# Decayed linear attention and two expert layers on one core: whole chunks of 128 on the halves of the TensorE array, operands in PSUM, and the first expert tile transposed earlier

## The chip, the cores and the metric

One Trainium2 chip, one of its cores. The metric is the device time of one execution of the whole program in microseconds; the kernel before was timed in three runs. TensorE (PE) multiplies, its weight loads are listed as PEld; VectorE is DVE, ScalarE is ACT, GpSimd is POOL, SyncE is SP. Each engine works through its own queue in order. Almost all transfers are issued from SP's queue; the indexed gathers and scatters from POOL's.

## The reference

Three stages follow each other. The inputs are 4 sequences x 8 heads x 768 tokens x 48 features.

```
state = alpha[t][:, None] * state + k[t][:, None] * v[t]     # per head, 48 x 48, token by token
y[t]  = q[t] @ state
x = y, heads side by side                                    # 3072 x 384
# first expert layer: every token goes to one of 8 experts
e = argmax(x @ w_gate + bias[modality]);  g = softmax weight of e
x = g * (relu(x @ w1[e]) @ w2[e])                            # 384 -> 1024 -> 384
# second expert layer: only tokens with x @ w_skip > 0
out = x + (relu(x @ w1b[e2]) @ w2b[e2])                      # else out = x
```

## The kernel before

**Attention.** The 3,072 tokens are 24 chunks of 128 (`SPB` = 6 to a sequence). The decay is turned into a running product `b` over the chunk (`scan`), so that a chunk needs only matrix products: `qmul` is q times b, and `lnexp`, `kmul`, `newton` and `kb` give k divided by b (the reciprocal by `Ln` and `Exp` on ScalarE and one Newton step on VectorE). Features lie on partitions, one head of a pair on 0 to 47 (`EV`), the other on 64 to 111 (`OD`), four pairs (`g`) side by side, so that every such operation has 128 partitions x 512 elements. `scores` multiplies kb with qb in two halves of 64 tokens, `masks` zeroes what lies ahead in time, `umm` gives the update of the state (to 64 and to 128 tokens), `state` subtracts it, `decay` multiplies by the chunk's last b, `scopy` copies the states. `ymm` forms y of 64 tokens in one product: the masked scores and the scaled q lie above each other in X and Y, v and the state in RX and RY; that is why v is also loaded a second time in another order (`vy`). `yout` copies y and stores it, `xpose`, `xcopy`, `logits` and `lgcopy` make the gate's logits of the first expert layer.

**The order.** The program is scheduled by hand: `FIRST` lists the calls of the first chunks, and `BODY` the calls of one step t, where `("scores", 2, 0)` works on chunk t-2. There are 22 listed steps (t from 4 to 25) and a tail written out behind them. An engine's queue holds its instructions in that order.

**Sort steps.** In the background of attention the tokens are sorted by expert, in batches of columns (a column is one chunk's 128 tokens): `BATCH1` gives first column, number of columns and the step at which a batch is put on the list. A batch chooses the expert of each token, ranks the tokens (`rank`), computes gate weights and builds two one-hot matrices for each column (`onehot`), whose product (`place`) writes the token numbers into the expert's rows of a table. Each `("tick",)` in `BODY` runs the list on by one `yield`, mostly one small VectorE instruction. `early` reads the table after the first batches, `early_rows` gathers the first tile's 256 rows.

**Weights.** `split` separates the fp32 weights of the first expert, loaded during attention, into a high part (ScalarE copy) and a low part (a subtraction); `side` does an eighth in a step. **Expert layers.** A branch (`ok_reg`) stands behind the attention, with a plain version of it that these inputs don't need. Then a loop over tiles of 256 tokens: gather, six transposes, split of the rows into high and low part (`lp.xpose`), three products for each of w1 and w2, scatter to `out` and `x2_d`. In its first tile the last batch of the sort runs in the background (`rest`, `turns`). The second layer works on tiles of 128.

Of the kernel before, what the change touches and what calls it, by code (L numbers as in the profile page):

```python
# [38 lines left out]
BODY = [
    ("ktr", 2), ("scan", 0), ("kcopy", 2), ("load_v", 0), ("decay",), ("kmul", 1), ("newton", 1), ("xpose", 4), ("load", -2), ("warm",),  # L40
    ("scores", 2, 0), ("xcopy", 4), ("qmul", 1), ("tick",), ("umm", 2), ("tick",), ("scores", 2, 1), ("guards", 1), ("ymm", 3, 0),
    ("lnexp", 0), ("state", 2), ("kb", 1), ("tick",), ("ymm", 3, 1), ("side", True), ("masks", 2, 0), ("masks", 2, 1), ("scopy", 2),
    ("logits", 4), ("yout", 3), ("tick",), ("start", -1), ("tick",), ("side", False), ("tick",), ("lgcopy", 4), ("hook",),
# [3 lines left out]
    ("load", 0), ("zero", "wz"), ("zero", "D1[0]"), ("warm", 12), ("clear", 0), ("load", 1), ("hook", -1), ("load_v", 0),  # L47
    ("zero", "D1[1]"), ("load", 2), ("start", 0), ("scan", 0), ("zero", "guard"), ("zero", "ups"), ("clear", 1), ("decay", -1),
    ("lnexp", 0), ("kmul", 0), ("newton", 0), ("kb", 0), ("start", 1), ("scan", 1), ("qmul", 0), ("clear", 2), ("warm", 5), ("ktr", 0),
    ("kcopy", 0), ("scores", 0, 0), ("load", 3), ("lnexp", 1), ("scores", 0, 1), ("masks", 0, 0), ("load_v", 1), ("umm", 0), ("qmul", 1),  # L50
    ("load_v", 2), ("kmul", 1), ("newton", 1), ("kb", 1), ("masks", 0, 1), ("state", 0), ("start", 2), ("scan", 2), ("warm", 6),
    ("load", 4), ("ktr", 1), ("decay", 0), ("kcopy", 1), ("scopy", 0), ("lnexp", 2), ("scores", 1, 0), ("scores", 1, 1), ("umm", 1),
    ("qmul", 2), ("zero", "m1"), ("zero", "wg"), ("guards", 2), ("masks", 1, 0), ("gate",), ("guards", 1), ("masks", 1, 1), ("ymm", 0, 0),
    ("kmul", 2), ("newton", 2), ("ymm", 0, 1), ("kb", 2), ("start", 3), ("guards", 0), ("load_v", 3), ("load", 5), ("state", 1),
# [6 lines left out]
def attention(tc, ctx, qka, vn, vy, wg1, x_d, ident, mask, lg, guard, ups, wz, hook, side, tick):  # L61
# [81 lines left out]
    def scores(i, c):
        if c == 0:
            st[i]["sc"] = ps.tile([P, NP, 2, CH], F32, name="sc")
        sc = st[i]["sc"]
        cs = slice(c * CH, c * CH + CH)
        for g in range(NP):
# [1433 lines left out]
```

## Time and profile before

| | |
|---|---|
| median of 3 runs | 651.57 us (650.91 to 653.29) |
| profiled execution, own time | 654.04 us |
| its span, first to last instruction | 652.3 us |
| PE busy | 589.5 us (90%) |
| DVE busy | 415.7 us (64%) |
| ACT busy | 286.1 us (44%) |
| POOL busy | 321.9 us (49%) |
| mean granted TensorE clock | 0.967 |

The attention takes the first 200 us or so, the first expert layer the stretch to about 475 us, the second the rest. Shares over the whole span mix three stages with different limits; the table is only the frame.

### The profile page before, as it was taken

How to read it: one execution, taken by the hardware profiler on the slowest of the kernel's cores; microseconds unless marked ns; L12 is line 12 of the kernel's file. 1: busy time of each engine (PE TensorE's matmuls, PEld its weight loads, DVE VectorE, ACT ScalarE, POOL GpSimd, SP SyncE). 2: the span in 40 equal slices, each digit the busy share in tenths (PEclk: the TensorE clock that was granted, in tenths of full speed). 3: DMA queues.
4: the chain of work that ended last, by engine and by line, in shares of the span. 5: the costliest groups of instructions: out<-in, count | busy, mean ns of one | idle time of the engine just before them, and what ended most of it. 6: DMA issues, size and time to landing. Idle time of an engine off the chain costs nothing. (4 is left out here: it accounts for less than half of the span.)

```text
span 652.3 us, 16532 instructions
## 1 busy us (share of the span) xinstructions
PE 589.5 (90%) x5491; PEld 539.5 (83%) x5498; DVE 415.7 (64%) x965; ACT 286.1 (44%) x563; POOL 321.9 (49%) x336
## 2 busy tenths in 40 slices
PE   6779897877897899999999999999879999999994
PEld 3668776776786799999999999999868878888894
DVE  8999999999967632454483443434476657547531
ACT  2756576656623122222442223222442838357521
POOL 5767687557624323424274432245335556437432
PEclk8978999989979899999999999999999999999998
DMA  8866799977511262214276422233001394807010
GB/s 263 203 148 160 173 272 309 209 197 196 160 34 35 55 226 73 72 38 143 66 228 206 134 68 68 76 116 106 28 15 46 124 307 165 302 30 236 28 34 26
DMA packets 42927, 87.64 MB, mean 134 GB/s; under 512 B 10032, under 2 KB 29714, under 8 KB 42788
## 3 DMA queue, kind: packets, MB, share of 16 engines
q1 hardware_dynamic: 35364, 65.87, 35.8%
q0 software_dynamic: 7424, 20.25, 9.2%
q8 instruction: 47, 0.77, 0.5%
q14 instruction: 92, 0.75, 0.4%
HBM read 65.86 MB, written 22.84 MB: 136 GB/s over the span
## 5 line engine op out<-in xcount | busy, mean ns | idle before, releaser
L797 PE MATMUL yp<-w2h,l_hh 128*128 128x384 f32 x336 | 102.3, 351 | 0.0
L1279 PE MATMUL hp<-l_x,w1h 128*128 128x256 f32 x624 | 99.9, 285 | 0.1
L797 PE MATMUL yp<-w2l,l_hh 128*128 128x384 f32 x336 | 98.7, 340 | 0.0
L797 PE MATMUL yp<-w2h,l_hl 128*128 128x384 f32 x336 | 98.2, 340 | 0.0
L1285 DVE SCALAR_TENSOR_TENSOR l_hl<-hp,l_hh 128x512 fp32r<-128x512 f32 x52 | 35.7, 686 | 88.8 <-ACT l_hh L1284 53.5
L1279 PEld LDWEIGHTS hp<-l_x,w1h 128*128 128x128 f32 x624 | 84.9, 190 | 0.7 <-issue 0.5
L710 POOL DMA_INDIRECT x_d<-ys,ti x24 | 25.1, 1046 | 100.9 <-DVEq L1230 55.5
L1284 ACT ACTIVATE l_hh<-hp 128x512 fp32r<-128x512 f32 x52 | 31.1, 599 | 92.9 <-PE hp L1279 79.8
L797 PEld LDWEIGHTS yp<-w2h,l_hh 128*128 128x128 f32 x336 | 61.0, 190 | 2.1 <-ACT l_hh L702 0.9
L797 PEld LDWEIGHTS yp<-w2h,l_hl 128*128 128x128 f32 x336 | 62.7, 190 | 0.0
L797 PEld LDWEIGHTS yp<-w2l,l_hh 128*128 128x128 f32 x336 | 60.9, 188 | 0.1
L1412 PE MATMUL hp<-w1h,l_x 128*128 128x512 f32 x192 | 54.0, 403 | 2.9 <-ACTq L1363 2.8
L1341 ACT ACTIVATE ys<-yp,l_gt 128x384 f32<-128x384 f32 x26 | 15.2, 584 | 89.3 <-PE yp L797 30.0
L1279 PE MATMUL hp<-l_x,w1l 128*128 128x256 f32 x312 | 53.9, 281 | 0.0
L201 PE MATMUL yp<-RX,X 128*64 128x48 f32 x384 | 47.3, 237 | 0.1
L703 DVE TENSOR_TENSOR l_hl<-tp,l_hh 128x512 fp32r<-128x512 f32 x32 | 22.1, 691 | 38.7 <-ACT l_hh L702 35.2
L202 PE MATMUL yp<-RY,Y 128*64 128x48 f32 x384 | 46.3, 232 | 0.0
L1415 ACT ACTIVATE hs<-hp 128x512 f32<-128x512 f32 x32 | 19.2, 599 | 60.3 <-PE hp L1412 60.1
L149 PE MATMUL sc<-X,kb 64*64 64x64 f32 x384 | 34.1, 234 | 12.2 <-DVE Y L155 10.5
L1279 PEld LDWEIGHTS hp<-l_x,w1l 128*128 128x128 f32 x312 | 44.5, 190 | 0.0
L149 PEld LDWEIGHTS sc<-X,kb 64*64 64x64 f32 x384 | 28.0, 144 | 19.9 <-POOL X L123 12.6
L123 POOL TENSOR_TENSOR Y<-qka,bt 48x512 f32<-48x512 f32 x24 | 43.4, 1807 | 1.8
(263 smaller groups left out, 1433.0 us busy)
## 6 DMA issues: line engine op xcount, KB each, us to landing
qka<-in_qka_dram SPq DMA_DIRECT2D x40, 288.0 KB
ring<-in_w1b_dram SPq DMA_DIRECT2D x5, 1536.0 KB
ring<-in_w2b_dram SPq DMA_DIRECT2D x5, 1536.0 KB
x_d<-xg SPq DMA_DIRECT2D x12, 385.0 KB
vn<-in_vn_dram SPq DMA_DIRECT2D x24, 192.0 KB
x_d<-xs SPq DMA_DIRECT2D x24, 192.0 KB
ring<-in_w2b_dram SPq DMA_DIRECT2D x4, 768.0 KB
qka<-in_qka_dram SPq DMA_DIRECT2D x3, 768.0 KB
```

What stands on the lines that cost most here:

```text
L123: nc.gpsimd.tensor_tensor(out=T[i % 4][r], in0=st[i]["q"][r], in1=st[i]["b"][r], op=MUL)
L149: nc.tensor.matmul(sc[OR:P, g, c], lhsT=st[i]["kb"][:OR, g, cs], rhs=X[i % 4][:OR, g, cs], start=True, stop=True)
L201: nc.tensor.matmul(yp[cs, 2 * g], lhsT=X[i % 4][:, g, cs], rhs=RX[i % 4][:, c, g], start=True, stop=True)
L202: nc.tensor.matmul(yp[cs, 2 * g + 1], lhsT=Y[i % 4][:, g, cs], rhs=RY[i % 4][:, c, g], start=True, stop=True)
L703: nc.vector.tensor_tensor(out=lo, in0=src, in1=hi.bitcast(F32), op=SUB)
L710: nc.gpsimd.indirect_dma_start(out=out, out_offset=bass.IndirectOffsetOnAxis(ap=idx, axis=0), in_=rows, in_offset=None, bounds_check=N - 1 ...
L797: nc.tensor.matmul(yp, lhsT=h[:, f, js], rhs=w[:, f], start=(f, i) == (0, 0), stop=(f, i) == last)
L1279: nc.tensor.matmul(hp[:, g], lhsT=w[:, c, f * P : (f + 1) * P], rhs=x[:, c], start=(i == 0), stop=(i == len(terms) - 1))
L1284: nc.scalar.activation(lp.hh[:, fs], hp, AF.Relu)
L1285: nc.vector.scalar_tensor_tensor(out=lp.hl[:, fs], in0=hp, scalar=0.0, in1=lp.hh[:, fs].bitcast(F32), op0=MAX, op1=SUB)
L1412: nc.tensor.matmul(hp[g], lhsT=a, rhs=b, start=(i == 0), stop=(i == 3 * DC - 1))
L1415: nc.scalar.activation(hs[:, g * 512 : (g + 1) * 512], hp[g], AF.Relu)
```

## The change

The attention works on whole chunks of 128 tokens. `scores` is eight products of 48 x 128 by 48 x 128, the even head of a pair on rows 0 to 63 of the array and the odd one on rows 64 to 127, and one mask product of 1,024 elements follows. y is formed transposed, with features on partitions, in one PSUM bank `yT`: `yheld` multiplies the held state with qb, `yadded` adds v times the masked scores. The gate's logits are taken from there (`logits` in four column groups, `ltcopy`, and `lturn`, which sums the four and turns them), and `xpose` turns y back into rows for storing. X, Y, RX, RY, the second copy of v, `clear` and `scopy` are gone; `umm` and `state` are made once for the chunk. `D1` and `r0` lie in PSUM, each with one buffer, `newton` writes over `r0`, and `kmul` is on VectorE. Logits go into the bank that also holds `ups`.

The order in `BODY` is new. One-hot matrices have 8 buffers, and `place` no longer runs within the ticks: columns are collected and multiplied by `("place",)` a step later; a batch pauses (`STEP`) until the next step after its count. The batches are 8, 8, 6 and 2 columns. `early` needs the first 8 alone. The batch of 6 is only ranked within attention, its one-hots are made in `rest`, ahead of the batch of 2. The low parts of the splits go to GpSimd, and `side` covers 16 eighths of w1 and w2. The first expert tile is transposed and split in the attention's tail (`first_rows`), ahead of the branch. `x2_d` is `x_d`, without the zero fill.

```
-WARM = (12, 5, 6, 8, 4, 2, 2) + (0,) * 18 + (2, 0, 0)
+WARM = (12, 5, 6, 8, 4, 2, 2) + (0,) * 21
 BODY = [
...
+    ("warm",), ("scores", 2), ("place",), ("qmul", 1), ("side", False), ("scan", 0), ("ktr", 2), ("kcopy", 2), ("load_v", 0), ("state", 3),
+    ("decay",), ("logits", 4), ("ltcopy", 4), ("kmul", 1), ("newton", 1), ("kb", 1), ("load", -2), ("yheld", 3), ("guards", 1), ("xpose", 4),
+    ("lturn", 4), ("yout", 4), ("lgcopy", 4), ("tick",), ("tick",), ("umm", 2), ("lnexp", 0), ("masks", 2), ("tick",), ("tick",), ("tick",),
+    ("tick",), ("yadded", 3), ("start", -1), ("side", True), ("ycopy", 3), ("hook",), ("done", 4),
 ]
...
-    D1 = bufs("D1", [P, NP, P], 2)
-    RX, RY = bufs("RX", [P, 2, NP, DH], 4), bufs("RY", [P, 2, NP, DH], 4)
+    D1 = ps.tile([P, NP, P], F32, name="D1")
+    yT = ps.tile([P, NP, P], F32, name="yT")
...
-        for R, r in ((RX, slice(OR, P)), (RY, slice(0, OR))):
-            nc.sync.dma_start(out=R[i % 4][r].rearrange("p c g e -> p (c g e)"), in_=vy[i, r])
...
-        r0 = st[i]["r0"] = wk.tile([P, NP, P], F32, name="r0")
+        r0 = st[i]["r0"] = ps.tile([P, NP, P], F32, name="r0")
...
-        (nc.vector if i < 3 else nc.gpsimd).tensor_tensor(out=k0, in0=st[i]["k"], in1=st[i]["r0"], op=MUL)
+        nc.vector.tensor_tensor(out=k0, in0=st[i]["k"], in1=st[i]["r0"], op=MUL)
...
-        for T, r in ((X, EV), (Y, OD)):
-            nc.gpsimd.tensor_tensor(out=T[i % 4][r], in0=st[i]["q"][r], in1=st[i]["b"][r], op=MUL)
+        t = st[i]["qb"] = wk.tile([P, NP, P], F32, name="qb", bufs=4)
+        nc.gpsimd.tensor_tensor(out=t, in0=st[i]["q"], in1=st[i]["b"], op=MUL)
...
-        nt = st[i]["nt"] = wk.tile([P, NP, P], F32, name="nt")
-        nc.vector.tensor_tensor(out=nt, in0=st[i]["b"], in1=st[i]["r0"], op=MUL)
+        nc.vector.tensor_tensor(out=st[i]["r0"], in0=st[i]["b"], in1=st[i]["r0"], op=MUL)
...
+    HEADS = [(g, par, (EV, OD)[par]) for g in range(NP) for par in range(2)]
+    def scores(i):
+        sc = st[i]["sc"] = ps.tile([P, 2, NP, P], F32, name="sc")
+        for g, par, d in HEADS:
+            nc.tensor.matmul(sc[:, par, g], lhsT=st[i]["kb"][d, g], rhs=st[i]["qb"][d, g], start=True, stop=True)
+    def masks(i):
+        t = st[i]["A"] = wk.tile([P, 2 * NP, P], F32, name="A")
         nc.vector.tensor_tensor(
+            out=t, in0=st[i]["sc"].rearrange("p r g t -> p (r g) t"), in1=mask.unsqueeze(1).to_broadcast([P, 2 * NP, P]), op=MUL
         )
...
+        for g, par, d in HEADS:
+            nc.tensor.matmul(up[d, g], lhsT=kbt[:, g, d], rhs=v[:, par, g], start=True, stop=True)
...
+    def yheld(i):
+        for g, par, d in HEADS:
+            nc.tensor.matmul(yT[d, g], lhsT=st[i]["S"][d, g], rhs=st[i]["qb"][d, g], start=g == 0, stop=False)
+    def yadded(i):
+        for g, par, d in HEADS:
+            nc.tensor.matmul(yT[d, g], lhsT=st[i]["v"][:, par, g], rhs=st[i]["A"][:, par * NP + g], start=False, stop=g == NP - 1)
+    def ycopy(i):
+        t = st[i]["yt"] = wk.tile([P, NP, P], F32, name="yt")
+        nc.scalar.copy(t[:DR], yT[:DR])
...
+            nc.tensor.matmul(lpt[32 * g : 32 * g + E], lhsT=wg[:DR, g], rhs=st[i]["yt"][:DR, g], start=True, stop=True)
+    def ltcopy(i):
+        t = st[i]["lt"] = wk.tile([P, P], F32, name="lt")
+        nc.scalar.copy(t, lpt)
+    def lturn(i):
+        nc.tensor.matmul(st[i]["xq"][:, 0, DR : DR + E], lhsT=st[i]["lt"], rhs=fold, start=True, stop=True)
...
-        for e, T, r in ((nc.gpsimd, RX[i], slice(32, OR)), (nc.gpsimd, RY[i], slice(96, P)), (nc.vector, X[i], slice(32, OR)), (nc.vector, Y[i], slice(96, P))):
-            e.memset(T[r], 0.0)
...
     a, z = NS - 2, NS - 1
+    place()
+    logits(a)
...
+    tick(8)
+    w = ps.tile([P, 2, NP, P], F32, name="sc")
+    first_rows([flat(w[:, r]) for r in range(2)])
...
-BATCH1 = ((0, 8, 13), (8, 8, 19), (16, 4, 24), (20, 4, NCOL + 4))
-EARLY = 2
+BATCH1 = ((0, 8, 12), (8, 8, 20), (16, 6, 25), (22, 2, NCOL + 4))
+EARLY = 1
...
-    x2_d = dr.tile([N, XW], F32, name="x2_d")
+    x2_d = x_d
...
-            while work:
+            while work and not held:
                 try:
-                    next(work[0])
+                    if next(work[0]) == STEP:
+                        held.append(1)
                     break
...
+    def places():
+        held.clear()
+        while columns:
+            place1(columns.pop(0))
...
-        if FT + 5 <= t < FT + 13:
-            wt.split(0, wt.one, parts=(t - FT - 5,), of=8, pool_parts=(), high=high, low=not high)
+        i = t - FT - (5 if high else 6)
+        if 0 <= i < 16:
+            wt.split(i // 8, wt.one, parts=(i % 8,), of=8, pool_parts=range(8), high=high, low=not high)
...
-        if 12 <= t < 24:
-            i = 2 * (t - 12)
-            nc.sync.dma_start(out=x2_d.rearrange("(p n) d -> p n d", p=P)[:, i : i + 2], in_=xg[1])
...
+            yield from onehots1(*BATCH1[-2][:2])
+            steps = batch(*BATCH1[-1][:2], [t[:, :64], tot])
...
-        lp.xpose(0, meanwhile)
-        wt.split(1, wt.one, parts=(1, 2), pool_parts=range(3))
+        turns(TU1)
+        i = NCOL + 1 - FT - 5 - 8
+        wt.split(1, wt.one, parts=(i,), of=8, pool_parts=range(8), high=False)
+        wt.split(1, wt.one, parts=range(i + 1, 8), of=8, pool_parts=range(8))
         turns(TU2)
```

## Rows read from the trace of the kernel before

**Rows 1.** Busy us (instructions) in stretches: PE, PEld, DVE, ACT, POOL; clock, DMA.

```profile
40.00:60.00 20.00, 17.63 (x271) 15.90 (x273) 18.46 (x24) 13.29 (x32) 14.70 (x12) 0.74 0.56 135
100.00:120.00 20.00, 16.55 (x302) 14.76 (x301) 19.88 (x39) 13.20 (x31) 13.70 (x10) 0.91 1.01 274
208.00:228.00 20.00, 17.24 (x116) 16.40 (x117) 14.32 (x59) 4.33 (x9) 9.80 (x10) 0.91 0.21 44
228.00:248.00 20.00, 20.00 (x151) 19.84 (x150) 6.31 (x24) 5.28 (x11) 5.26 (x9) 1.00 0.56 207
```

**Rows 2.** Single lines, 60 to 160 us: ns minimum/median/maximum, first and last start.

```profile
L102 DVE TENSOR_SCALAR D<-qka x13: 152/281/1262, 66.9 to 155.4; 128x4 f32<-128x4 f32 x13
...
L106 DVE TENSOR_TENSOR_SCAN bt<-qka,D x13: 1204/1212/2306, 67.2 to 158.0; 128x512 f32<-128x512 f32 x13
...
L127 DVE TENSOR_TENSOR nt<-bt,r x14: 654/660/1701, 59.7 to 159.2; 128x512 f32<-128x512 f32 x14
...
L132 DVE SCALAR_TENSOR_TENSOR kb<-nt,k x13: 673/683/1562, 62.1 to 153.0; 128x512 f32<-128x512 f32 x13
...
L155 DVE TENSOR_TENSOR X<-sc,call x13: 695/695/695, 64.4 to 153.9; 64x512 f32<-64x512 f32 x13
```

**Rows 3.** Order in time, GpSimd and VectorE: start us, us, instruction.

```profile
107.10 1.27 POOL L123 TENSOR_TENSOR X<-qka,bt 48x512 f32<-48x512 f32 x1
...
107.15 1.26 DVE L102 TENSOR_SCALAR D<-qka 128x4 f32<-128x4 f32 x1
```

**Rows 4.** Order in time, VectorE: the sixth and the last scan of 24.

```profile
38.41 1.22 DVE L106 TENSOR_TENSOR_SCAN bt<-qka,D 128x512 f32<-128x512 f32 x1
...
172.74 1.22 DVE L106 TENSOR_TENSOR_SCAN bt<-qka,D 128x512 f32<-128x512 f32 x1
```

**Rows 5.** Costliest groups: count, busy us, mean ns of one, idle before.

```profile
L1285 DVE SCALAR_TENSOR_TENSOR l_hl<-hp,l_hh 128x512 fp32r<-128x512 f32 x52 | 35.7, 686 | 88.8 <-ACT l_hh L1284 53.5 <-ACTq L1230 34.4 <-issue 0.9
```

**Rows 6.** Order in time, VectorE: one pair of one-hots.

```profile
181.72 0.27 DVE L527 TENSOR_SCALAR s_S<-call,s_lo 128x128 f16<-128x128 f32 x1
181.92 0.36 DVE L529 TENSOR_SCALAR s_R<-call,s_col 128x192 f16<-128x192 f32 x1
```

**Rows 7.** Order in time, TensorE: scores, y, gate, transposes, and last the update product.

```profile
102.13 0.27 PE L149 MATMUL sc<-X,kb 64*64 64x64 f32 x1
...
102.59 0.22 PE L149 MATMUL sc<-X,kb 64*64 64x64 f32 x1
...
103.24 0.28 PE L201 MATMUL yp<-RX,X 128*64 128x48 f32 x2
...
103.48 0.32 PE L201 MATMUL yp<-RX,X 128*64 128x48 f32 x4
...
103.75 0.28 PE L201 MATMUL yp<-RX,X 128*64 128x48 f32 x2
...
104.55 0.94 PE L221 MATMUL xq<-wg1s,xt 128*128 128x128 f32 x6
105.55 0.57 PE L137 MATMUL kp<-call,kb 112*128 112x112 f32 x4
...
190.82 1.06 PE L169 MATMUL sb<-vn,kbt 64*48 64x48 f32 x32
```

**Rows 8.** Groups of ScalarE: a copy of the states (RY's is the second).

```profile
L188 ACT COPY RX<-S 48x384 f32<-48x384 f32 x24 | 12.2, 507 | 9.3 <-DVE S L174 9.3
```

**Rows 9.** Groups of VectorE: one of the two clears of a buffer.

```profile
L230 DVE MEMSET X<- 32x512 f32 x4 | 1.9, 485 | 0.6 <-issue 0.5
```

**Rows 10.** Order in time behind attention: the branch, the first tile, the second's transposes.

```profile
204.79 0.19 DVE L988 TENSOR_TENSOR s_L<-lg,sel 128x32 f32<-128x32 f32 x1 [2.07 <-DVEq L1081]
...
208.00 0.59 PE L1279 MATMUL hp<-l_x,w1h 128*128 128x256 f32 x3
...
214.45 0.24 PE L533 MATMUL acc<-s_R,s_S 128*128 128x192 f16 x1 [2.01 <-DVE s_R L529]
...
225.99 0.82 PE L776 MATMUL px<-call,xg 128*128 128x128 f32 x6
```

More of the change, by code (lines that the diff above doesn't have):

```diff
@@ L44 @@
 ]
 FIRST = [
[L47 to L54, printed above, removed]
@@ L55 @@
-    ("yout", 0), ("scopy", 1), ("scan", 3), ("clear", 3), ("warm", 8), ("lnexp", 3), ("hook", 0), ("start", 4),
+    ("load", 0), ("zero", "wz"), ("zero", "D1"), ("warm", 12), ("load", 1), ("hook", -1), ("load_v", 0),
+    ("load", 2), ("start", 0), ("scan", 0), ("zero", "guard"), ("zero", "ups"), ("zero", "yT"), ("decay", -1),
+    ("lnexp", 0), ("kmul", 0), ("newton", 0), ("kb", 0), ("start", 1), ("scan", 1), ("qmul", 0), ("warm", 5), ("ktr", 0),
+    ("kcopy", 0), ("scores", 0), ("load", 3), ("lnexp", 1), ("masks", 0), ("load_v", 1), ("umm", 0), ("qmul", 1),
@@ new lines @@
+    ("load_v", 2), ("kmul", 1), ("newton", 1), ("kb", 1), ("state", 0), ("start", 2), ("scan", 2), ("warm", 6),
+    ("load", 4), ("ktr", 1), ("decay", 0), ("kcopy", 1), ("lnexp", 2), ("scores", 1), ("umm", 1),
+    ("qmul", 2), ("zero", "m1"), ("zero", "wg"), ("guards", 2), ("masks", 1), ("gate",), ("guards", 1), ("yheld", 0), ("yadded", 0),
+    ("kmul", 2), ("newton", 2), ("kb", 2), ("start", 3), ("guards", 0), ("load_v", 3), ("load", 5),
+    ("ycopy", 0), ("scan", 3), ("warm", 8), ("lnexp", 3), ("hook", 0), ("start", 4),
@@ L143, in scores @@
[L143 to L148, printed above, removed]
-            nc.tensor.matmul(sc[OR:P, g, c], lhsT=st[i]["kb"][:OR, g, cs], rhs=X[i % 4][:OR, g, cs], start=True, stop=True)
-            nc.tensor.matmul(sc[:OR, g, c], lhsT=st[i]["kb"][OR:, g, cs], rhs=Y[i % 4][OR:, g, cs], start=True, stop=True)
-    def masks(i, odd):
-        T, r = ((X, slice(OR, P)), (Y, slice(0, OR)))[odd]
+        nc.scalar.copy(t, st[i]["kp"][:, :, :DR])
@@ L249, in gate @@
     def gate():
-        nc.sync.dma_start(out=wg[:, :, :E], in_=wg1.rearrange("(c p) e -> p c e", p=P))
+        w = wg1.rearrange("(g r e) n -> r e g n", r=2, e=DH)
+        for par, d in enumerate((EV, OD)):
+            nc.sync.dma_start(out=wg[d], in_=w[par])
     for e in FIRST:
         dict(locals())[e[0]](*e[1:])
-    base = dict(ktr=2, kcopy=2, scan=0, lnexp=0, start=-1, load=-2, load_v=0, xpose=4)
-    ops = dict(ktr=ktr, kcopy=kcopy, scan=scan, lnexp=lnexp, start=start, load=load, load_v=load_v, kmul=kmul, newton=newton, scores=scores, ymm=ymm, umm=umm, guards=guards, kb=kb, qmul=qmul, logits=logits, state=state, scopy=scopy, yout=yout, masks=masks, lgcopy=lgcopy, xpose=xpose, xcopy=xcopy)
+    base = dict(ktr=2, kcopy=2, scan=0, lnexp=0, start=-1, load=-2, load_v=0, ycopy=3)
+    ops = dict(ktr=ktr, kcopy=kcopy, scan=scan, lnexp=lnexp, start=start, load=load, load_v=load_v, kmul=kmul, newton=newton, scores=scores, yheld=yheld, yadded=yadded, umm=umm, guards=guards, kb=kb, qmul=qmul, logits=logits, state=state, ycopy=ycopy, yout=yout, masks=masks, lgcopy=lgcopy, ltcopy=ltcopy, lturn=lturn, xpose=xpose, done=done)
     for e in BODY:
@@ L279, in attention @@
     a, z = NS - 2, NS - 1
+    place()
+    logits(a)
+    ltcopy(a)
+    yheld(z)
     xpose(a)
-    xcopy(a)
-    ymm(z, 0)
-    ymm(z, 1)
-    yout(z)
-    warm(TAIL[0])
-    logits(a)
-    lgcopy(a)
-    hook(NS + 2)
-    tick(nt)
-    xpose(z)
-    xcopy(z)
-    warm(TAIL[1])
-    logits(z)
-    lgcopy(z)
-    tick(nt)
+    lturn(a)
+    yadded(z)
+    lgcopy(a)
+    yout(a)
+    ycopy(z)
+    tick(8)
+    w = ps.tile([P, 2, NP, P], F32, name="sc")
+    first_rows([flat(w[:, r]) for r in range(2)])
+    hook(NS + 2)
+    logits(z)
+    ltcopy(z)
+    xpose(z)
+    lturn(z)
+    lgcopy(z)
+    place()
+    tick(8)
+    yout(z)
     hook(NS + 3)
@@ L706 @@
 ET = mybir.EngineType
+STEP = "step"
 def put(nc, out, idx, rows):
@@ L1050, in hook @@
             first_loads()
+        if t == NCOL + 1:
+            check.append(fast_ok(one))
+            next(check[0])
         if t == NCOL + 2:
-            fast_ok(one)
+            now(check[0])
         if t == NCOL + 3:
```

185 lines of the change are left out of this document (81 added, 104 removed).

## The prediction

> **What bounds the kernel now.** I read the stretches first, then single lines, then the order in time. In the attention steps VectorE is the full engine: 19.88 of 20 us, with TensorE at 16.55, ScalarE at 13.20 and GpSimd at 13.70; from 208 us on TensorE is full and VectorE is at a third [rows 1]. So until about 200 us a microsecond off VectorE counts, and afterwards only TensorE's time does.
>
> Next is what VectorE does with its time. The same instruction has a minimum and a maximum far apart: the 4-element start 152 to 1262 ns, the scan 1204 to 2306, `newton`'s product 654 to 1701, `kb` 673 to 1562. The mask product, whose one operand is in PSUM, took 695 ns thirteen times out of thirteen [rows 2]. The order in time shows the cause: GpSimd's `qmul` began at 107.10 and took 1.27 us; VectorE's start began at 107.15 and ended 0.04 us after it [rows 3]. An instruction that takes all its operands from SBUF stands still while GpSimd works; one with a PSUM operand does not. The sixth scan begins at 38.41 us and the last at 172.74: 18 steps in 134.3 us, 7.46 us each [rows 4].
>
> **VectorE's part of a step.** D1 and r0 move to PSUM, so start, scan, `kmul`, `newton` and `kb` each keep at most one SBUF input. I price them at their undisturbed times: start 0.15, scan 1.21, `newton` and `kb` 0.69 each [rows 2]. 0.69 is also what the 512-element product on a PSUM operand takes in the expert stage [rows 5]. `kmul` comes from GpSimd: plus 0.69. The two mask products become one of 1,024 elements: 0.69 + 512 more at (0.695 - 0.152)/508 = 1.07 ns each = 1.24. Of the two state subtractions one stays: 192 elements, 0.15 + 0.20 = 0.35. Sum 0.15 + 1.21 + 3 x 0.69 + 1.24 + 0.35 = 5.0 us. Bounds of the PSUM form: not dearer than the minimum (4.9 in all), or the mask's 35 ns over `newton`'s minimum on each of the five (5.2). I take 5.0.
> [...]
>
> Between these sit the sort's small steps: 16 one-hot pairs at about 0.49 from start to start [rows 6], some 50 others near 0.2 (estimate; none is longer than a one-hot undisturbed). About 14 us of them fall into the 18 steps, some 9 of which carry them: +1.5 us there, and +0.3 where GpSimd still holds one of them up. VectorE then needs 5.0 (4.6 to 5.0, since starts overlap ends by 0.07) in an empty step and 6.4 in a loaded one. The weight splits' low halves go to GpSimd, hidden: it then has `qmul` 1.27, decay and one split of 384 elements, about 3 us of a step (an estimate).
>
> **TensorE's part.** Each fp32 matmul is two records. In scores two quadrants run at once: 8 pairs in 0.46 us, 0.066 a pair [rows 7]. With 128 columns a pair takes 0.13: scores 1.05, `yheld` the same 1.05. The update product halves, 1.06 to 0.53. Two sets of four transposes: 2 x 0.57. `lturn` 0.25 (estimate: two of the gate products' 0.125). Gate product now: six of 128 columns in 0.94, so (0.94 - 0.32)/5 = 0.125 each, with 0.32 the length of one. `yadded` streams 128 columns through 48 weight columns, 16 x 0.125 = 2.0 us one after the other, or 1.0 if the even and odd heads' column halves overlap. One place shows such an overlap: where the first column half meets the second, 8 records take 0.27 us, against 4 in 0.24 just before [rows 7]. The new gate products go to four column groups: 8 x 0.125 = 1.0, or 0.25. Sum 1.05 + 1.05 + 0.53 + 1.14 + 0.25 + (1.0 to 2.0) + (0.25 to 1.0) = 5.3 to 7.0 us, against 16.55/20 x 7.46 = 6.2 now. I take 5.9, near the overlapped end, because rows show overlap in both directions.
> One wait is new here. The gate products write the bank that `state` reads, so `logits` of chunk t-4 waits until `state` of chunk t-3 is done, 1.6 us into VectorE's step. Behind it in TensorE's order stand `yheld`, the transposes, `lturn`, `umm` and `yadded`, 4.0 us at the chosen rates: they end 5.6 us into the step, and the next scores need the mask before them anyway. It hides in a step of 6 us and sets the floor at about that; I put empty steps at 6.0.
>
> **ScalarE's part** is now 13.20/20 x 7.46 = 4.9 us [rows 1]. The state copies (2 x 0.51) and one more copy of 384 elements, as long, go [rows 8]; a copy of 512 elements (0.65 by length), one of 128 (0.2) and half a microsecond of high split more often come, estimates by length: about 4.8. r0 has one buffer now, so `Ln` of chunk t waits for `kb` of chunk t-1, 3.6 us into the step; behind it on ScalarE are the high split and `ycopy`, for which only the next step's gate product waits. `Ln` and `Exp` end at 3.7 + 1.26 = 5.0, and `kmul` asks for them at one step + 1.6: hidden while a step is above 3.5 us.
>
> **Sum of the steps.** Empty steps at that 6.0, loaded ones at VectorE's 6.4, mean 6.2; +0.2 because the clock is at its lower level in parts (0.74 in one stretch [rows 1]) and TensorE has less slack to hide it. 18 x (7.46 - 6.4) = **19 us**.
>
> **Startup.** The eight VectorE clears (0.485 each [rows 9] and up to 0.15 until the next, 5 us), one D1 memset (0.5) and some 4 us of stretched operations (an estimate: four that take the maxima of [rows 2] for the minima) go; yT's memset (0.5) and two `kmul` (1.4) come: **7.5 us**. `load_v`'s two extra transfers leave SP's queue, which nothing waited for; counted at nothing. So do the twelve zero fills.
>
> **Step 23 to the first expert product**: now 208.00 - 172.74 = 35.3 us [rows 4, 10]. After: rest of step 23 6.4; step 24, with no scan but 12 sort steps, 6.4; step 25 to its mask 2.8; then VectorE has 8 one-hot operations (2.2), 8 ranking steps (1.7), the first tile's two low halves (1.1), and count to gate weights (2.5): 7.5; the branch 2.07 [rows 10]. Total 25.2: **10 us** less. The six transposes of the first tile, after the branch now, stand ahead of it.
>
> **First expert tile**, 208.00 to 225.99. It waits 2.01 us for a one-hot operation that GpSimd's weight split holds up, and at 0.91 of the clock loses 1.8 us [rows 1, 10]. GpSimd's share drops from two parts of 1,024 elements to about three of 384. But eight columns' one-hots (before: four) now come in the background, some 8 steps later, so the index is ready about 3 us later and the gather of the second tile may show. Net **3 us**, bounds 0 and 4.
>
> **No change elsewhere**: 13 first-layer and 16 second-layer tiles. With the first batch alone (1,024 tokens) the first expert needs 256 tokens; the reference's own inputs route 483 there, so no tile is added. x2 shares x's rows now; gather and scatter of one tensor are ordered among each other, but stand several us apart on GpSimd's queue.
>
> Sum: 19 + 7.5 + 10 + 3 = 39.5. Against the profiled execution's 654.04 that is 614.5; the median of the runs is 2.5 lower, so **612 us**.
>
> **Rivals.**
> *TensorE becomes the bound* (column halves do not overlap): 7.0 a step instead of 6.4, 18 x 0.6 = 11 us, 623. The single place of overlap in the rows is thin evidence: 0.22.
> [...]
> *The second tile's gather is late*: `placed` runs 8 steps longer, 3 us of index plus two gathers; the first tile gains nothing and loses 4 more: 619. 0.10.
> *Nothing is gained on VectorE*, that is, GpSimd holds up PSUM forms too: a step is 7.46 - 0.34 - 0.15 + 0.69 (+ up to 0.5) = 7.7 to 8.2, 4 to 13 us lost in the steps, 20 gained around them: 635 to 644. Against it: thirteen masks without a spread; for it: no scan with a PSUM operand is shown. 0.08.
> [...]
> [...] 0.04.
> My forecast holds 0.56. Slower by over 0.5% (what a measurement of this kernel can just tell from no change) comes from the last rival alone, same from the edge of the one before: faster 0.93, same 0.03, slower 0.04.
>
> **Range.** Lower end: TensorE at 5.3 and VectorE never held up, 5.7 a step: 18 x 0.7 = 12.6 less, 600. Upper end: TensorE at 7.0 and the gather late: 623 + 7 = 630.
>
> **What would show it.** Scans at 1.21 without spread; steps of 6.2 to 6.6 us; masks as one operation of 1.24; the last scan near 146 us, the first expert product near 171, the second tile's transposes near 186; 13 and 16 tiles. Wrong, if TensorE is full from 30 to 150 us, if VectorE's forms with PSUM still spread, or if the second tile waits for its rows.

## The result and the profile after

The changed kernel takes 618.63 us (median of 4 runs, 617.63 to 619.74), the kernel before 651.24 on the same chip (649.91 to 653.29): a ratio of 0.9497 (95% interval 0.9465 to 0.9529). The forecast was 612.0, its range 600 to 630. The profiled execution took 617.63 us (span 615.9, mean granted clock 0.974), 36.4 less than the profiled one of before. One execution of the study, the profiled one of `rows_behind_branch`, was a slow one and is not counted in its ratio (with it the median of its four runs is 614.01 us). By the places at which the prediction cut the program (only the fourth stretch ends later than there, behind the second tile's transposes and not ahead of them):

| stretch | before | after | gained | predicted |
|---|---|---|---|---|
| start to the sixth scan | 38.41 | 27.24 | 11.2 | 7.5 |
| sixth scan to the last, 18 steps | 134.33 | 107.79 | 26.5 | 19 |
| last scan to the first expert product | 35.26 | 30.53 | 4.7 | 10 |
| to the second half of the first tile's second products | 18.56 | 22.08 | -3.5 | 3 |
| the rest | 425.7 | 428.3 | -2.5 | 0 |

The forecast of the median is 6.6 us off. The sum is 3.1 us off (39.5 predicted, 36.4 measured) because errors of 2.5 to 7.5 us in all five terms nearly cancelled. The other 3.5 us come from the profiled executions: the prediction put the median 2.5 us under the profiled execution, and after the change it lies 1.0 above it. What has to be explained is the terms.

The scans that bound the 18 steps, in the order of time of VectorE after (against [rows 4]):

```profile
27.24 1.21 DVE L101 TENSOR_TENSOR_SCAN bt<-qka,D 128x512 f32<-128x512 f32 x1
...
135.03 1.22 DVE L101 TENSOR_TENSOR_SCAN bt<-qka,D 128x512 f32<-128x512 f32 x1
```

The busy time by stretches after, columns as in [rows 1]:

```profile
40.00:60.00 20.00, 19.41 (x316) 15.99 (x314) 18.65 (x37) 13.66 (x38) 7.01 (x10) 1.00 0.91 206
...
100.00:120.00 20.00, 19.73 (x307) 16.66 (x306) 19.55 (x38) 14.85 (x40) 8.23 (x10) 0.93 0.73 167
...
160.00:180.00 20.00, 12.65 (x85) 11.63 (x85) 13.64 (x59) 3.61 (x9) 3.85 (x4) 0.66 0.09 15
```

TensorE and VectorE are now both nearly full in the steps, and GpSimd's 13.7 us of 20 have become 8. The third line is the branch and most of the first expert tile: no engine is full there, and the clock is at 0.66 on average: it is granted at 0.50 from 162 to 174 us and at 1.00 from 176 us on.

Single VectorE lines after, 27 to 160 us, minimum, median and maximum in ns (against [rows 2]):

```profile
L97 DVE TENSOR_SCALAR D<-qka x18: 153/156/168, 31.7 to 134.8; 128x4 f32<-128x4 f32 x18
...
L101 DVE TENSOR_TENSOR_SCAN bt<-qka,D x19: 1214/1221/1222, 27.2 to 135.0; 128x512 f32<-128x512 f32 x19
...
L122 DVE TENSOR_TENSOR r<-bt,r x20: 686/690/692, 29.2 to 141.7; 128x512 f32<-128x512 f32 x20
...
L127 DVE SCALAR_TENSOR_TENSOR kb<-r,k x20: 691/692/692, 29.9 to 142.4; 128x512 f32<-128x512 f32 x20
...
L154 DVE TENSOR_TENSOR A<-sc,call x21: 1197/1215/1221, 30.5 to 149.4; 128x1024 f32<-128x1024 f32 x21
```

The spread is gone: minimum and maximum lie within 25 ns, where they lay up to 1.1 us apart. An empty step in TensorE's order after (against [rows 7]):

```profile
60.67 1.16 PE L149 MATMUL sc<-qb,kb 48*128 48x128 f32 x16 [0.54 <-DVE D L97]
61.76 0.60 PE L133 MATMUL kt<-call,kb 112*128 112x112 f32 x4
62.31 0.41 PE L202 MATMUL sb<-yt,wg1s 112*8 112x128 f32 x8
62.65 1.08 PE L180 MATMUL yT<-qb,S 48*48 48x128 f32 x16
63.66 0.60 PE L133 MATMUL kt<-call,yt 112*128 112x112 f32 x4
64.10 0.30 PE L210 MATMUL kt<-call,lt 128*128 128x8 f32 x2
64.33 0.56 PE L161 MATMUL sb<-vn,kbt 128*48 128x48 f32 x16
64.72 1.05 PE L185 MATMUL yT<-A,vn 128*48 128x128 f32 x16
```

From 60.67 to the next scores at 65.70 TensorE never stops: 5.0 us a step, where the prediction took 5.9. Around the branch after, in TensorE's order (against [rows 10]):

```profile
159.06 0.40 PE L202 MATMUL sb<-yt,wg1s 112*8 112x128 f32 x8 [2.30 <-DVE nok L957]
...
165.56 0.98 PE L1310 MATMUL hp<-l_x,w1h 128*128 128x256 f32 x3 [5.13 <-DVEq L1107]
...
169.47 0.32 PE L525 MATMUL acc<-s_R,s_S 128*128 128x192 f16 x1 [1.14 <-DVE s_R L521]
...
187.12 0.76 PE L768 MATMUL px<-call,xg 128*128 128x128 f32 x5 [1.01 <-DMA xg<-x_d,l_gi]
```

The last gate product waits 2.30 us for the capacity check `nok`, whose sum lies in its PSUM bank; TensorE then stands 5.13 us before the branch; in the tile it waits for one-hots, and at the end for the second tile's rows.

### The profile page after: what moved, and what is told of

Read it like the earlier page. It is cut to its first block, busy times and chain, and to the rows that moved or that the text cites. A ratio compares the mean times of both kernels' runs of the same rounds, so it can differ in the third digit from the quotient of the medians.

```text
span 615.9 us, 14961 instructions
## 1 busy us (share of the span) xinstructions
PE 568.7 (92%) x4836; PEld 510.9 (83%) x4836; DVE 366.2 (59%) x923; ACT 264.3 (43%) x544; POOL 248.0 (40%) x296
## 5 line engine op out<-in xcount | busy, mean ns | idle before, releaser
L1310 PE MATMUL hp<-l_x,w1h 128*128 128x256 f32 x624 | 102.4, 290 | 5.1 <-DVEq L1107 5.1
L1310 PEld LDWEIGHTS hp<-l_x,w1h 128*128 128x128 f32 x624 | 86.9, 194 | 5.4 <-issue 5.4
L694 DVE TENSOR_TENSOR l_hl<-tp,l_hh 128x512 fp32r<-128x512 f32 x32 | 22.1, 691 | 39.0 <-ACT l_hh L693 35.4
L711 POOL DMA_INDIRECT xg<-x_d,l_gi x31 | 32.0, 1031 | 31.8 <-PE hp L1310 14.8
L1444 PEld LDWEIGHTS hp<-w1h,l_x 128*128 128x128 f32 x192 | 35.7, 188 | 10.7 <-ACTq L1395 3.2
L119 POOL TENSOR_TENSOR qb<-qka,bt 128x512 f32<-128x512 f32 x24 | 30.6, 1273 | 16.0 <-DVE k L115 6.1
L694 DVE TENSOR_TENSOR l_x<-px,l_x 128x384 fp32r<-128x384 f32 (+2 forms) x43 | 22.8, 554 | 21.5 <-ACT l_x L693 10.6
L1444 PE MATMUL hp<-w1l,l_x 128*128 128x512 f32 x96 | 29.9, 408 | 4.2 <-DVE w1l L388 4.0
```

Of the source, the lines that this page charges most:

```text
L119: nc.gpsimd.tensor_tensor(out=t, in0=st[i]["q"], in1=st[i]["b"], op=MUL)
L694: nc.vector.tensor_tensor(out=lo, in0=src, in1=hi.bitcast(F32), op=SUB)
L711: nc.gpsimd.indirect_dma_start(out=xg[:, j, :], out_offset=None, in_=src, in_offset=bass.IndirectOffsetOnAxis(ap=gi[:, j : j + 1], axis=0) ...
L1310: nc.tensor.matmul(hp[:, g], lhsT=w[:, c, f * P : (f + 1) * P], rhs=x[:, c], start=(i == 0), stop=(i == len(terms) - 1))
L1444: nc.tensor.matmul(hp[g], lhsT=a, rhs=b, start=(i == 0), stop=(i == 3 * DC - 1))
```

## The experiments

Each kernel is the changed one with one edit (a few carry two or three, as said there), compared with the kernel before on its own chip. Ratios are to be read beside the 0.9497 (0.9465 to 0.9529) of the changed kernel.

### Operands back in SBUF

```
-    D1 = ps.tile([P, NP, P], F32, name="D1")
+    D1 = keep.tile([P, NP, P], F32, name="D1")
```

> One tile back: D1, the scan's and the start's second operand, lies in SBUF again, as in the kernel before; all else stays. Theory (GpSimd holds up a VectorE instruction that takes all its operands from SBUF, and the PSUM operand is what freed the scan): start and scan spread again, the scan from 1.22 us to 1.9 or more in many of the 18 steps (GpSimd now works about 40% of a step), 0.3 to 0.45 us a step on average, 5 to 8 us in all: 624 to 627 us. Rival (where the operand lies is of no matter; the steps are shorter because there are fewer operations, clears and transfers): scans stay at 1.22 and the time at 618 to 619 us.

Measured: 619.81 us (618.55 to 623.01), ratio 0.9524 (0.9494 to 0.9555), not told apart from the changed kernel. Of 24 scans five were stretched (1.55 to 2.12 us), the others took 1.22 to 1.23. So the scan is held up again, as the theory says, but too seldom for its price of 5 to 8 us. With this edit in place, r0 goes back as well:

```
-        r0 = st[i]["r0"] = ps.tile([P, NP, P], F32, name="r0")
+        r0 = st[i]["r0"] = wk.tile([P, NP, P], F32, name="r0")
```

> Two tiles back in SBUF: D1 and r0 (with two buffers, as before), so start, scan, kmul, newton and kb take all their operands from SBUF; all else stays. Theory (GpSimd holds them up): all five spread; with the 0.3 to 0.45 us of start and scan some 0.7 to 1.1 us a step, 13 to 20 us over 18 steps: 632 to 639 us. Rival (placement is of no matter): 618 to 619 us; and r0's second buffer, which takes away the wait of Ln for the chunk before, would then show as a gain of up to 1 us.

Measured: 648.15 us (645.03 to 651.28), ratio 0.9962 (0.9940 to 0.9984): nearly the whole gain is gone, 0.4% of the time is left of it. 21.6 us are lost in the 18 steps (129.4 against 107.8), more than the 13 to 20 that the theory expected. The rival is out. The line of `newton` in this kernel, and VectorE and GpSimd in one of its steps:

```profile
L122 DVE TENSOR_TENSOR r<-bt,r x18: 692/2111/2120, 32.5 to 151.3; 128x512 f32<-128x512 f32 x18
```

```profile
76.71 0.83 POOL L174 TENSOR_TENSOR S<-T,bt 112x192 f32<-112x192 f32 x1 [4.21 <-DVE T L167]
77.20 2.12 DVE L122 TENSOR_TENSOR r<-bt,r 128x512 f32<-128x512 f32 x1
77.50 1.27 POOL L119 TENSOR_TENSOR qb<-qka,bt 128x512 f32<-128x512 f32 x1
```

`decay` and `qmul` follow each other on GpSimd without a gap, and `newton`, 0.69 us long, ends 0.55 us after the second of them. In the new order GpSimd's two operations fall on `newton` in nearly every step, and seldom on the scan: what `newton` takes beyond 0.69 us adds up to 18.4 of the 21.6 us. So r0's move to PSUM is worth most of the gain in the steps, and D1's little by itself (r0 alone in SBUF was not run).

### TensorE's halves one after the other

```
-        for g, par, d in HEADS:
+        for g, par, d in sorted(HEADS, key=lambda h: h[1]):
             nc.tensor.matmul(yT[d, g], lhsT=st[i]["v"][:, par, g], ...
```

> Only the order of yadded's 16 products changes: the eight of the even heads, then the eight of the odd ones, so that neighbours write the same 48 of the 128 columns of the array and cannot run at once; same products, same results. Both theories: yadded goes from 1.05 to about 2.0 us. Theory of the prediction (TensorE sets the length of an empty step): each step 0.5 to 1.0 us longer, 9 to 18 us, 628 to 637 us. Rival (a step is set by VectorE and by waits, TensorE has slack): under 0.2 us a step, 618 to 622 us.

Measured: 626.33 us (625.57 to 626.80), ratio 0.9633 (0.9610 to 0.9657). TensorE's order in this kernel:

```profile
62.79 1.16 PE L149 MATMUL sc<-qb,kb 48*128 48x128 f32 x16
...
66.83 1.52 PE L185 MATMUL yT<-A,vn 128*48 128x128 f32 x16
68.28 1.16 PE L149 MATMUL sc<-qb,kb 48*128 48x128 f32 x16
```

The time lies between the two expected ranges. The same 16 products take 1.52 instead of 1.05 us, not 2.0, and TensorE's empty step becomes as much longer: 5.49 (62.79 to 68.28) instead of 5.03. The 18 steps take 113.2 us, 5.4 more. So the overlap of the column halves is real and used, and longer TensorE work shows in the steps: the changed kernel, in which VectorE needs 4.7 from scan to scan and TensorE 5.0 from scores to scores, stands at that edge. The mechanism is the one the prediction gave to its first rival.

### The second copy of v

```
         nc.sync.dma_start(out=t.rearrange("p r g e -> p (r g e)"), in_=vn[i])
+        again = wk.tile([P, 2, NP, DH], F32, name="vy", bufs=2)
+        for r in (slice(OR, P), slice(0, OR)):
+            nc.sync.dma_start(out=again[r].rearrange("p r g e -> p (r g e)"), in_=vn[i, r])
```

> The two extra transfers per chunk that the change took out of load_v come back: v is loaded a second time in two halves of the partitions, into a tile that nobody reads. Theory (nothing waited for them; counted at nothing in the prediction): 618 to 620 us, the sixth scan at 27 us still. Rival (they stood on SP's queue ahead of the loads that the startup waits for; the startup's surplus of 4 us over the prediction came from them): the sixth scan 1 to 4 us later, 620 to 623 us.

Measured: 627.44 us (624.75 to 631.79), ratio 0.9634 (0.9589 to 0.9680), 8.8 us more than the changed kernel by the medians (4 to 14 by the ends of the intervals) and more than either side expected. In its profiled execution, the longest of its four (631.79 us), the 18 steps take 117.0 us, 9.2 more; in five other kernels here with the same attention (`warm_tail`, `tail_split_dve`, `check_later`, `combined`, `x2_apart`) they took 107.1 to 108.0, and 111.5 in the profiled execution of `rows_behind_branch`. The sixth scan begins 2.3 us later, but among kernels whose start is the same it lies anywhere from 27.2 to 29.4 us. VectorE's order in this kernel:

```profile
79.12 0.17 DVE L100 TENSOR_SCALAR D<-qka 128x4 f32<-128x4 f32 x1 [2.54 <-DMA qka<-in_qka_dram]
...
92.01 0.17 DVE L100 TENSOR_SCALAR D<-qka 128x4 f32<-128x4 f32 x1 [2.20 <-DMA qka<-in_qka_dram]
```

The next chunk's rows come late. To tell bytes from the number of transfers, the same two transfers with 8 of 384 columns:

```
+            nc.sync.dma_start(out=again[r].rearrange("p r g e -> p (r g e)")[:, :8], in_=vn[i, r, :8])
```

> As in v_twice, two more transfers per chunk on SP's queue, in the same places, but each takes only 8 of the 384 columns (2 KB instead of 96 KB). This tells apart why the full second copies of v cost 8.8 us. If it is the bytes (the transfer engines are busy 0.87 to 0.96 of the stretch from 20 to 100 us in the kernel after, and VectorE waited 5.9 us for rows of q, k and a with the second copies): 618 to 620 us, no wait of VectorE for such rows after 27 us. If it is the number of transfers or their issue on SP's queue: 625 to 628 us as before.

Measured: 619.58 us (617.14 to 620.75), ratio 0.9509 (0.9474 to 0.9545), 18 steps in 108.5 us. So it is not the number of the transfers. (VectorE's waits for such rows did not go to nothing, which the side of the bytes had expected: 3.7 us in three places, against 5.9 with the full copies and none in the changed kernel.) Nor are bytes alone enough: `x2_apart`, below, moves as many more and loses nothing. The queue that carries them, in the changed kernel, `v_twice` and `x2_apart` (packets, MB, and their time as a share of the span of 16 engines):

```profile
q1 hardware_dynamic: 29812, 56.46, 32.5%
```

```profile
q1 hardware_dynamic: 33652, 61.18, 34.9%
```

```profile
q1 hardware_dynamic: 31540, 61.19, 34.0%
```

By these shares the second copies of v hold all 16 engines for 20 us more than in the changed kernel, the fills for 9. Why the one delays the rows that VectorE needs and the other does not is open. The transfer engines of the changed kernel are busy 0.91, 0.96 and 0.90 of the time in the three stretches of 20 us from 40 to 100 us, so there is little room.

### Around the branch

Four edits for the 22 us tile and the 30.5 us ahead of it. In the attention's tail:

```
     tick(8)
+    warm(12)
     yout(z)
```

> Twelve idle products (bf16, 512 columns, on zeros, 0.24 us each at full clock) are added to TensorE behind the last gate product, where it stands idle for 5.1 us before the branch; nothing reads them. In the kernel after, the granted clock is at half from about 160 to 174 us, that is through most of the first expert tile. Theory (that tile came out at 21.6 instead of the predicted 15 us above all for the clock): the clock stays full there, the stretch from the first expert product to the second tile's transposes falls from 21.6 to about 18, total 615 to 616 us. Rival (the tile waits for one-hot operations on VectorE, which run no faster with TensorE's clock): under 1 us, 618 us.

Measured: 619.70 us (616.25 to 620.65), ratio 0.9462 (0.9403 to 0.9521); the tile 23.0 us. Windows of the changed kernel, and below of this one:

```profile
160.00:170.00 10.00, 3.51 (x19) 2.74 (x18) 5.92 (x18) 1.71 (x5) 3.58 (x4) 0.54 0.16 29
170.00:180.00 10.00, 9.14 (x66) 8.89 (x67) 7.72 (x42) 1.90 (x4) 0.26 (x1) 0.78 0.02 2
```

```profile
160.00:170.00 10.00, 6.82 (x40) 3.96 (x41) 4.15 (x18) 2.28 (x7) 0.96 (x2) 0.83 0.12 27
170.00:180.00 10.00, 7.26 (x41) 6.65 (x40) 7.04 (x30) 1.21 (x3) 2.65 (x3) 0.66 0.05 4
```

Against the changed kernel the time is not told apart. The time at the lower clock moved, it did not go: 0.54 and 0.78 became 0.83 and 0.66. Behind the branch TensorE starts at full clock (1.00 from 167 to 171 us) but now waits 3.4 us for one-hots (2.2 before this edit), and the clock falls there (0.60 from 171 to 175 us, 0.54 from 175 to 179). That is the rival: the one-hots on VectorE do not come sooner. What the tile would take at full clock throughout, this run does not show.

```
-        wt.split(1, wt.one, parts=(i,), of=8, pool_parts=range(8), high=False)
-        wt.split(1, wt.one, parts=range(i + 1, 8), of=8, pool_parts=range(8))
+        wt.split(1, wt.one, parts=(i,), of=8, pool_parts=(), high=False)
+        wt.split(1, wt.one, parts=range(i + 1, 8), of=8, pool_parts=())
```

> The low halves of the second layer's weight splits behind the branch go from GpSimd to VectorE; all else stays. Theory (GpSimd's three splits, 2.98 us from 167.3 us on, hold up VectorE's one-hot operations there, which TensorE waits for: 0.75 to 1.06 us each instead of about 0.23): one-hots at 0.23 to 0.3, waits of TensorE for them (1.14, 0.90 us) gone, 2 to 3 us less: 615.5 to 616.5 us. Rival (the splits then take as long on VectorE, ahead of the same one-hots): no change or 1 us more, 618 to 620 us.

Measured: 616.36 us (614.54 to 617.56), ratio 0.9430 (0.9378 to 0.9483). The splits take 1.48 us on VectorE instead of 2.98 on GpSimd, and the stretched one-hots behind them are gone, but the tile is only 0.4 us shorter (21.7). The interval overlaps that of the changed kernel: a gain of 2 us is possible and not shown.

```
-    hook(NS + 2)
     logits(z)
...
     lgcopy(z)
+    hook(NS + 2)
```

> The capacity check (the hook that ends in nok) is issued behind the last chunk's gate logits instead of ahead of them; nothing else moves. Theory (the 2.30 us for which the last gate product waits for nok, because both use one PSUM bank, lie on the path to the branch): the wait is gone, the stretch from the last scan to the first expert product falls from 30.5 to about 28.5 us. Rival (VectorE has to do the check before the branch anyway, so it only comes later): 30 to 31 us.

Measured: one run, 618.33 us. The 2.30 us are gone, and last scan to first expert product takes 29.7 us instead of 30.5: nearer to the rival's 30 to 31 than to the theory's 28.5, and one run does not decide on 0.8 us. The three together, with one more sort step at a place (`TU3` 4 for 3):

> The three edits of warm_tail, tail_split_dve and check_later together, and four instead of three sort steps at one place of the first tile. If the three waits are separate and each lies on the path: 2 us from the check, 3 to 4 us from clock and one-hots together (they overlap in the same tile), 611 to 614 us. If what goes comes back as another wait (the gather of the second tile, 1.0 us of which TensorE waits for now): 616 to 618 us.

Measured: 616.98 us (614.86 to 620.34), ratio 0.9437 (0.9374 to 0.9500): the rival's range, and no more than `tail_split_dve` alone.

Then the early transposing itself, undone:

```
-    w = ps.tile([P, 2, NP, P], F32, name="sc")
-    first_rows([flat(w[:, r]) for r in range(2)])
...
-        turns(TU1)
+        lp.xpose(0, lambda: turns(TU1))
```

> The transposes of the first tile's rows and their split into high and low halves go back behind the branch, as in the kernel before; all else stays. Theory (they fill waits ahead of the branch, and behind it they stand on the path): they take 3.2 us from the branch to the first expert product in the kernel before, so 2 to 3.2 us more: 620.5 to 622 us. Rival (the work only moves, because VectorE is on the path ahead of the branch too): within 1 us, 618 to 619.5 us.

Measured: ratio 0.9401 (0.9358 to 0.9444), 610.68 to 615.98 us in the three runs that it rests on. This is faster than the changed kernel, with intervals that do not meet: 1% by the middles, 0.2% by the nearest ends. Neither side expected that sign. There is a profile only of its execution of 622.93 us, so the stretches below show where that execution differs; that the gain of the three runs lies there is likely and not shown. From the end of the steps (the last mask product) to the branch, and from there to the second half of the second products, first the changed kernel, then this one:

```profile
149.45:165.57 16.12, 8.65 (x126) 6.86 (x122) 8.11 (x35) 4.95 (x14) 0.00 (x0) 0.85 0.15 41
165.57:187.64 22.07, 18.32 (x115) 16.60 (x116) 16.78 (x74) 4.00 (x8) 8.20 (x10) 0.80 0.12 25
```

```profile
157.77:171.18 13.41, 7.99 (x119) 6.18 (x115) 7.07 (x34) 3.99 (x12) 0.00 (x0) 0.88 0.17 50
171.18:192.00 20.82, 17.98 (x121) 16.33 (x122) 16.91 (x76) 4.75 (x10) 8.45 (x11) 0.91 0.13 27
```

With the transposes behind it the branch comes 2.7 us sooner (the first stretch takes 16.0 and 16.2 us in `tail_split_dve` and `x2_apart`), and the tile with them inside is not longer but 1.3 us shorter (22.1 us in the changed kernel, 21.8 to 23.5 in others with the same tile). VectorE ahead of the branch in the changed kernel:

```profile
157.30 0.69 DVE L694 TENSOR_TENSOR l_x<-sc,l_x 128x512 fp32r<-128x512 f32 x1 [2.17 <-ACT l_x L693]
158.43 0.43 DVE L694 TENSOR_TENSOR l_x<-sc,l_x 128x256 fp32r<-128x256 f32 x1 [0.44 <-ACT l_x L693]
...
160.53 0.23 DVE L502 TENSOR_TENSOR s_a<-sb,s_M 128x48 f32<-128x48 f32 x1 [1.62 <-ACT lg L213]
...
165.57 0.29 DVE L519 TENSOR_SCALAR s_S<-call,s_lo 128x128 f16<-128x128 f32 x1 [3.34 <-DVEq L1107]
```

It waits 2.6 us for ScalarE's half of the row split; the check and the last gate product queue behind that, and the branch comes last. Behind the branch TensorE waits for one-hots anyway (2.2 us in the changed kernel, 1.2 here), and the transposes take that time. How much of the tile's 1.3 us is its higher clock (0.91 against 0.80) stays open.

### Two more

`tail_split_dve` with the copy of the early table on VectorE, behind the index:

```
-        elif tab is not None:
-            nc.scalar.copy(tab, v)
...
+        if not more and tab is not None:
+            nc.vector.tensor_copy(tab, v)
```

> tail_split_dve, and the copy of the position table behind the early index goes from ScalarE to VectorE, behind the index instead of ahead of it. Theory (VectorE waits 1.84 us at 121.4 us because ScalarE, which is behind with other work, reads the same PSUM bank first): that wait goes, the copy costs about 0.35 us on VectorE, 1 to 1.5 us less than tail_split_dve's 616.4 us: about 615 us, and about 3.5 us under the kernel after. Rival (the early index has slack; the next step waits for something else there): 616 to 617 us.

Measured: 619.85 us (615.48 to 623.08, 6 runs), ratio 0.9500 (0.9462 to 0.9539). The wait of 1.84 us is gone and that step takes 6.0 instead of 7.7 us, but nothing is left of it: last scan to first expert product is 36.1 us in the profiled execution (622.84 us), whose clock is at 0.67 from 140 to 180 us. The total lies above what either side expected; why the clock fell is open.

```
-    x2_d = x_d
+    x2_d = dr.tile([N, XW], F32, name="x2_d")
...
+        if 12 <= t < 24:
+            i = 2 * (t - 12)
+            nc.sync.dma_start(out=x2_d.rearrange("(p n) d -> p n d", p=P)[:, i : i + 2], in_=xg[1])
```

> The second layer's rows get their own tensor again, with its twelve zero fills, as in the kernel before; all else stays. Question: from the second half of the first tile's second products to the end the kernel after takes 428.3 us, the kernel before 425.7. Theory (sharing x's rows orders gathers and scatters among each other and costs there): that stretch goes back to about 426, but the fills' twelve transfers of 385 KB cost in the steps, where transfers are already close to full: total 618 to 624 us. Rival (the 2.6 us are dips of the clock, one of 3.4 us near 300 us alone costs 1.7): the stretch stays at 426.5 to 428.5 us.

Measured: 617.44 us (616.45 to 619.60), ratio 0.9478 (0.9441 to 0.9516); steps 107.1 us, the rest 427.5. Sharing costs nothing that can be measured here, and the fills are hidden: the rival. The fastest kernel seen is the one with the rows behind the branch; with `tail_split_dve` added to it, it was not tried.

## Why the forecast held, term by term

The time fell into the range because errors of both signs nearly cancelled, and that is luck. What was right is the cause of the gain in the steps. Two of the prediction's own signs of being wrong came up as well: the second tile waits for its rows, and TensorE is busy 8.6 to 10 of every 10 us from 30 to 90 us.

**VectorE's 5.0 us a step was right**, in sum and in every row: 0.16 + 1.22 + 0.33 + 0.68 + 2 x 0.69 + 1.22 = 4.99. The cause was right too: with r0 and D1 back in SBUF GpSimd holds up `newton`, whose median is 2.111 us in `d1_r0_sbuf` instead of 0.690. The scans without a spread (1.214 to 1.222 us) agree. The operand in PSUM, for which the prediction's upper bound has 35 ns on each of five operations, cost 30 ns on `newton` (0.690 against 0.660 us) and 9 on the scan (1.221 against 1.212), by the medians of the changed kernel and of [rows 2]. Which operand carried the gain was not foreseen. The rival "nothing is gained on VectorE" is out.

**The step that failed most in the steps is "I put empty steps at 6.0".** They take 4.4 to 5.1 us. The terms were mis-sized: `yadded` at 1.05 and the gate products at 0.41 lie near the lower ends of their bounds, and the transposes and the update product take 1.0 and 0.39 from start to start where the sum has 1.14 and 0.53, so TensorE needs 5.0 and not 5.9, less than the lower bound of 5.3; and the new wait of `logits` for `state` does not add, because `yheld`, transposes and the rest behind it take 3.05 us (62.65 to 65.70) and not 4.0. The 0.2 us for the clock were hardly used: it is granted at 1.00 from 30 to 90 us. 18 x (6.4 - 5.99) = 7.4 us more gained than predicted. Most loaded steps came out at 5.6 to 6.5, up to what was predicted (6.4). Four take 7.6 to 9.3, which no term had: in three of them VectorE waits for ScalarE (0.88, 1.07 and 1.84 us), in the longest a sort step of 8 elements was held for 3 us. VectorE and GpSimd there, after:

```profile
129.21 2.98 DVE L535 SCALAR_TENSOR_TENSOR s_v<-s_rot,s_v 128x8 f32<-128x8 f32 x1
129.47 0.98 POOL L388 TENSOR_TENSOR w2l<-raw,w2h 128x384 fp32r<-128x384 f32 x1
130.42 0.50 POOL L174 TENSOR_TENSOR S<-T,bt 112x192 f32<-112x192 f32 x1
130.89 1.26 POOL L119 TENSOR_TENSOR qb<-qka,bt 128x512 f32<-128x512 f32 x1
```

**"Counted at nothing" was wrong for the transfers of v.** At 7.46 us a step VectorE waited for no transfer; at 6 us a step they would cost 8.8 by the medians (`v_twice`), and not by their number (`v_thin`). So with them in the queue the steps would not have come down as far. The zero fills were rightly counted at nothing (`x2_apart`).

**Startup: 11.2 gained, not 7.5.** The term that was mis-sized is the "some 4 us of stretched operations". Three of them, before:

```profile
27.55 2.32 DVE L106 TENSOR_TENSOR_SCAN bt<-qka,D 128x512 f32<-128x512 f32 x1
29.79 1.70 DVE L127 TENSOR_TENSOR nt<-bt,r 128x512 f32<-128x512 f32 x1
...
34.85 1.30 DVE L909 CAST triu<-call 128x128 bf16<-128x128 f32 x1
```

Ahead of the sixth scan ten VectorE operations took 8.6 us more before than their like in the changed kernel, where none is stretched. Against that stand 2.3 us of waits for the first rows after, in whose place VectorE cleared buffers before. The start also varies by 2 us from run to run, so the rest of the term is not told apart.

**Last scan to first expert product: 4.7 gained, not 10.** Predicted 25.2 us, measured 30.5. The part up to the last mask took 14.4 against 15.6 in the sum; from there to the branch it is 16.1 (with the mask's own 1.1) against 9.6. The failed step is that this sum adds up VectorE's operations alone and puts its waits at nothing: 2.6 us for ScalarE's half of the early rows' split, and 1.6 for the last gate logits. The rows' own split of 1.1 was in the sum. In the profile of `rows_behind_branch` 2.7 us come back, but with the rows away VectorE still waits 1.1 us for the check and 1.6 for the gate logits, so the early rows are one part of it. The branch itself cost 3.3 instead of 2.07 us of VectorE's time; why is open (3.2 with the rows behind it, so they are not the cause).

**First tile: 3.5 lost, not 3 gained.** The two gains that were counted did not come. "GpSimd's share drops" was true, and the one-hots still met its three splits: TensorE waits 2.2 us for them, where the prediction took 2.01 away. Nor did the clock's 1.8 us go: it is granted at 0.54 and 0.78 in the two windows under `warm_tail`, that is, with 0.50 as the lower level and 1.00 as the upper, (1 - 0.54) x 20 + (1 - 0.78) x 20 = 13.6 us at the lower one, some of them in the branch's idle time. A group of the tile's products at the lower level, and at the upper one in `warm_tail`:

```profile
171.99 0.84 PE L1310 MATMUL hp<-l_x,w1l 128*128 128x256 f32 x3
```

```profile
168.26 0.52 PE L1311 MATMUL hp<-l_x,w1l 128*128 128x256 f32 x3
```

Seven such groups, from start to start, take 2.2 us longer than at the upper level (an estimate from these two traces). The two losses cannot be added, since `warm_tail` shows that TensorE, when it is faster, waits longer for the one-hots. Only in the profile with the transposes behind the branch does the stretch come near that of before again (19.0 against 18.56). The rival of the late gather came true in part: TensorE waits 1.5 us for the second tile's rows.

**The rest: 2.5 us longer.** Not the shared rows (`x2_apart`). In the runs of this study, with the same code there, the stretch took 426.2 to 430.8 us; the 425.7 of before may be the edge of that spread. It stays open.

## What to carry to other kernels

Price a removed or kept transfer, and a floor, against the step length after the change, not the one before: here the second copies of v cost 8.8 us at steps of 6 us, and VectorE waited for no transfer at 7.46. Put the waits between engines into a sum of one engine's operations (2.6 and 1.6 us were missing here). What an operand's move to PSUM earned here is what GpSimd's operations fell on in the new order (`newton`, 18.4 of 21.6 us), so look at which instruction overlaps them before choosing the tile to move. Work drawn ahead of a branch was not free here: the check and the last gate product queued behind it, and the branch came 2.7 us later; in the waits behind the branch it may be cheaper (the tile was 1.3 us shorter in the one profile).

## What the runs showed of the hardware

VectorE instructions with all operands in SBUF were held over several GpSimd instructions that follow each other without a gap: 8 elements took 2.98 us under three of them, `newton` 2.12 under two. But three one-hots took 1.01, 1.06 and 1.01 us beside three splits without a gap, so each of them did get a turn:

```profile
168.35 1.06 DVE L521 TENSOR_SCALAR s_R<-call,s_col 128x192 f16<-128x192 f32 x1
```

```profile
167.28 2.98 POOL L388 TENSOR_TENSOR w2l<-raw,w2h 128x384 fp32r<-128x384 f32 x3
```

What tells the two cases apart is open; the held ones take two tiles, the one-hots one tile and a scalar for each partition. A PSUM operand cost almost nothing on VectorE: the scan took 1.221 us with it, and without it 1.212 [rows 2] and 1.23 (`d1_r0_sbuf`); `newton` took 0.690 against 0.660 [rows 2], and 0.692 from SBUF in the one step of `d1_r0_sbuf` where it was not held. Products that alternate between the column halves of the array took 0.066 us each, the same ones half by half 0.095, where 0.125 was expected. Twelve idle products ahead of the branch did not keep the clock up behind it: 0.83 and 0.66 were granted in the two windows from 160 to 180 us, against 0.54 and 0.78 without them.
